# Block-sparse attention with a rational feed-forward layer: the first loads in another order, the first sampled keys copied by the vector engine, and three more buffers for the first values

## The chip, the cores and the metric

The kernel runs on one core of a Trainium2 chip. The metric is the device time of one execution in microseconds (us); three executions of the kernel before gave 875.51, 877.20 and 879.96, so the median is 877.2 us. The core has a matmul engine (PE in the profile, with its weight loads as PEld), a vector engine (DVE), a scalar engine (ACT), a general engine (POOL), and the queue SP, which here issues every DMA.

## The reference

First comes attention over `q`, `k`, `v` of shape (4, 8, 768, 64): 4 batches, 8 heads, 24 blocks of 32 rows. A block of queries sees its own block, its two neighbours, the first, the last, and three sampled blocks (`sampled_blocks`, an input); the first and the last block see everything.

```
scores = where(mask, q @ k.T / sqrt(64), -1e9);  attn = softmax(scores);  x = (attn @ v) as 3072 x 512
h = x @ w_in                                     (512 x 2048)
g = (a0 + a1*h + a2*h^2 + a3*h^3) / (1 + |b0|*|h| + |b1|*h^2 + 1e-6)
out = g @ w_out                                  (2048 x 512)
```

All inputs are float32 but the weights and the small vectors of the second part, which are float64 and are turned into float32 on the chip with integer operations (shift, or) of the vector engine.

## The kernel before

**Tiling.** The 3072 rows of `x` are 12 chunks of 256 rows (8 blocks), three chunks for each batch. A chunk's attention is done block by block (a `part` per block; the first and the last block of a batch take three parts), and then the chunk goes through 8 `unit`s (L1132), each of 256 of the 2048 columns of `w_in`. A unit is 24 matmuls into `ph` (L1150 to L1152: high and low float16 halves of `x` and of the weights), a row of scalar and vector operations for the rational function, and matmuls into `acc` (L1206 to L1208). The units' order is written out: units 0 to 3 of chunk 0, all of chunk 1, units 4 to 7 of chunk 0, then the other chunks.

**The planner.** Every piece of work is an `Op` with an engine, a price, its predecessors, the buffers that it takes from a `Ring`, and a priority. `issue` (L161 to L279) runs the list as a small simulation and emits the instructions in the order that comes out: of the operations that could start at about the same time, the one with the lower priority number goes first. So a priority is a due time, and the order of each engine's queue and of SP's is fixed when the kernel is built. Where PE has nothing to do in the first stage, `fill` (L162) puts in matmuls of an identity matrix, whose result nobody reads.

**The start.** `prep(0, ...)` (L556) loads the keys of batch 0 (six pieces of 256 KB, L545), takes their largest absolute value with ACT (`bound`, L397), makes a power of two of it (`scales`, L341: a PE transpose, a reduction and four small DVE operations) and splits, transposes and stores the keys in `kall` (`rest`, L634). In the same call it loads the values of batch 0 (L590) and takes their maximum, because the first chunk's `x` is scaled by it before it is split into float16 halves. `prep_q` does the same for 128 queries at a time, out of one buffer `ldq`; the split queries `qa` are copied to the other half of the partitions by two DMAs (`qc`, L766, L767). The key and value maxima have priorities -83.96 and -78.19.

**A part of chunk 0 or 1** (`attention`, L833). `copies` (L861) reads three block numbers from `ix` into registers of ACT and copies those blocks of `kall` into `kxs` (L866); `scores` (L913), `maxima` (DVE, L923), `exps` (ACT, L941), `turn` (PE transposes, L982), `whole` (ACT or DVE, L150), and `values` (PE, L1039) follow. The part's values come from DRAM in `load` (L1003 the three neighbours, L1005 and L1006 the first and the last block, when the buffer doesn't hold them yet, and three DMAs of L1009 for the sampled blocks, whose numbers SP reads into registers, twelve numbers for four blocks at a time). There are three value buffers `vgs`, so the load of part x waits for the values of part x-3. After four blocks, `weigh` (L1073) and `turn_x` (L1085) make a piece of `x`, and `evac_high` (L150) and `evac_low` (L1097) split it.

**The weights.** `weights()` (L414) loads 512 KB pieces into two buffers `wl`. A piece takes a conversion (ACT, POOL or DVE), and three DVE operations `pack1` to `pack3` (L447, L450, L453). Four pieces make a group of `w_in` (two units); a group then has its own scale, and three operations for each piece make its high and low halves (L150, L154, L511). A group's pieces have the priority of its first unit less 4.91: for group 0 that is -4.91. Chunk 0's attention has priorities -19 to -12.8, the set-up -70.

Of the kernel before, what the change touches and what calls it, by code (L numbers as in the profile page):

```python
# [23 lines left out]
def kernel(  # L24
# [265 lines left out]
    ix = const.tile([1, NB, 4], I32, name="ix")  # L290

# [122 lines left out]
    def weights():  # L414
# [5 lines left out]
        for u in range(NG):  # L420
            pieces += [(min(place[0, 2 * u], place[1, 2 * u]) + -4.91, 0, u, x) for x in range(NCC)]
# [101 lines left out]
    vgs = [const.tile([P, 2, 2, 2, HG * D], F16, name=f"vg{i}") for i in range(3)]  # L523
    r_kg, r_vg = Ring(range(len(kgs))), Ring(range(len(vgs)))

# [22 lines left out]
    PLAIN = B  # L548
# [4 lines left out]
    def prep(b, when):  # L553


        kv[b] = [None] * 5  # L556
        s_scr[b] = Slot(r_ks)
        first = b == 0
        n = len(units)
        k_done[b], v_done[b] = [], []  # L560
        before = {}
        if first:
            rings = [[(r_tt, "tt", p2), (r_ab, "ab", p2), (r_sq, "sq", p2)], [(r_pr, "pr", p3), (r_ld, "ld", p3)]]
        for w in ([2] if b >= QB else []) + [0, 1]:
# [7 lines left out]
            for j in range(n):  # L572
                def one(j, w=w, lds=lds, mx_tile=mx_tile):
                    prio = when(w, 0, j)
                    if first:
                        ring, tag, pool = rings[w][j // (2 + w)]
                    else:
                        ring = r_ld
# [6 lines left out]
                    def load():  # L585
                        if first:
                            nb = {"tt": 3, "pr": 4}.get(tag)
                            d["ld"] = pool.tile([P, 512], F32, name=tag, bufs=nb)
                            if w:
                                nc.sync.dma_start(out=d["ld"], in_=v[b].rearrange("h (a r) d -> (h a) (r d)", a=P // H)[:, j * 512:(j + 1) * 512])  # L590
                            else:
                                load_unit(k, b, *units[j], d["ld"])
# [24 lines left out]
            def largest(mx=mx, w=w):  # L617
# [5 lines left out]
                           finish=out_scale if w and b < PLAIN else None)  # L623
            (k_scale, v_scale)[w][b] = o
            if w and b < PLAIN:
                continue
# [11 lines left out]
    def rest(b, w, j, d, o_scale, sc, prio, before):  # L638
# [25 lines left out]
        if w == 1:  # L664
            def store():
                if kv[b][1] is None:
                    kv[b][1] = scr.tile([S, H * 2 * D], F16, name="vs")
                n = HU * 2 * D
                nc.sync.dma_start(out=kv[b][1][t * CH:(t + 1) * CH, g * n:(g + 1) * n].rearrange("(p s) c -> p s c", s=2),
                                  in_=d["hl"].rearrange("p (s j) a d -> p s (j a d)", s=2))  # L670
            v_done[b].append(Op(SY, [(650, 262144)], store, [o], prio, uses=[s_hl, s_scr[b]]))
            return
# [40 lines left out]
    def prep_q(b, t, prio, before):  # L713
# [4 lines left out]
        s_ld, s_hl, s_ps = Slot(r_ldq), Slot(r_hlq), Slot(r_sp)  # L718
# [4 lines left out]
        def load():  # L723
            d["ld"] = p1.tile([P, 512], F32, name="ldq")
# [58 lines left out]
        x = Op(TE, 445, transposes, [l], prio, takes=[s_ps], uses=[s_hl])  # L783
        x = Op(SC, 904, evac, [x], prio, takes=[d["slot"]], uses=[s_ps])
# [12 lines left out]
    def sampled_rows(x, eng=mybir.EngineType.SP):  # L797

        b, j = parts[x][:2]
        i = block(j)  # L800
        if (b, i, eng) not in rows_of:
            some = [n for n in (block(m) for m in range(j - j % 4, j - j % 4 + 4)) if n not in (0, NB - 1)]
            values = nc.values_load_multi_w_load_instructions(
                ix[0:1, some[0]:some[-1] + 1, 0:NR], engines=[eng], min_val=0, max_val=NB - 1,
                skip_runtime_bounds_check_because="clamped when ix was written")[1]
            for n, m in enumerate(some):
                rows_of[b, m, eng] = values[n * NR:(n + 1) * NR]
# [310 lines left out]
    def factors(b, u, n, after, prio):  # L1118

        def run():  # L1120
            if b not in fcs:
                fcs[b] = p2.tile([P, 4, NU], F32, name="fc")
# [254 lines left out]
```

## Time and profile before

| what | value |
|---|---|
| median of 3 executions | 877.2 us (875.51 to 879.96) |
| profiled execution: its own time | 878.83 us |
| profiled execution: span from the first to the last instruction | 877.0 us |
| mean granted PE clock, as a share of full speed | 0.976 |
| busy PE, DVE, ACT, POOL | 825.4, 729.0, 675.4, 111.4 us |
| moved by DMA | 151.16 MB, 172 GB/s over the span |

A busy time is a share over stages with different limits, so the rows below are cut into stretches of the span. Time on PE includes the fills. "Idle before" is the time in which an engine did nothing ahead of an instruction, with what ended it.

### The profile page before, as it was taken

How to read it: one execution, taken by the hardware profiler on the slowest of the kernel's cores; microseconds unless marked ns; L12 is line 12 of the kernel's file. 1: busy time of each engine (PE TensorE's matmuls, PEld its weight loads, DVE VectorE, ACT ScalarE, POOL GpSimd, SP SyncE). 2: the span in 40 equal slices, each digit the busy share in tenths (PEclk: the TensorE clock that was granted, in tenths of full speed). 3: DMA queues.
4: the chain of work that ended last, by engine and by line, in shares of the span. 5: the costliest groups of instructions: out<-in, count | busy, mean ns of one | idle time of the engine just before them, and what ended most of it. 6: DMA issues, size and time to landing. Idle time of an engine off the chain costs nothing.

```text
span 877.0 us, 27047 instructions
## 1 busy us (share of the span) xinstructions
PE 825.4 (94%) x10334; PEld 644.6 (73%) x10334; DVE 729.0 (83%) x1731; ACT 675.4 (77%) x1447; POOL 111.4 (13%) x118
## 2 busy tenths in 40 slices
PE   8988687588899999999999999999999999999997
PEld 3545566366687888888788887878778888788886
DVE  5758987999998888888887877887878887778886
ACT  6777977797787897798777788998768687767563
POOL 1124622635220000000000000000000000000000
PEclk9999898699999999999999999999999999999999
DMA  7888689586765965889755976899555965630000
GB/s 201 209 158 209 194 177 199 127 238 196 203 156 152 273 203 157 210 214 241 200 146 139 241 204 190 198 248 248 152 131 162 224 170 160 183 102 26 1 25 25
DMA packets 240209, 151.16 MB, mean 172 GB/s; under 512 B 16208, under 2 KB 222928, under 8 KB 240080
## 3 DMA queue, kind: packets, MB, share of 16 engines
q1 hardware_dynamic: 240080, 149.43, 66.4%
q8 instruction: 82, 1.34, 0.7%
q14 instruction: 47, 0.39, 0.2%
HBM read 132.07 MB, written 11.01 MB: 163 GB/s over the span
## 4 chain that ended last, share of the span: by engine, by line
PE 69%; DVE 9%; DMA 9%; ACT 5%; SPq 4%; issue 3%; POOL 1%; ACTq 0%; DVEq 0%; POOLq 0%
PE acc L1206 9%; PE ph L1150 9%; PE acc L1208 8%; PE acc L1207 8%; PE ph L1152 8%; PE ph L1151 8%; PE av L1039 5%; PE pt L982 5%; PE sp L913 5%; DMA vg<-in_v_dram 2%; DMA wl<-in_moe_w_in_dram 2%; ACT pr L941 1%; DVE pr L923 1%; SPq L1009 1%; PE sp L758 1%
## 5 line engine op out<-in xcount | busy, mean ns | idle before, releaser
L1150 PE MATMUL ph<-xh,wi 128*128 128x256 f16 x768 | 212.1, 276 | 3.7 <-DVE tt L1167 3.6
L1152 PE MATMUL ph<-xh,wi 128*128 128x256 f16 x768 | 210.9, 275 | 0.5 <-POOL wi L511 0.5
L1151 PE MATMUL ph<-xl,wi 128*128 128x256 f16 x768 | 210.9, 275 | 0.0
L1206 PE MATMUL acc<-wo_h,gh 128*128 128x512 f32 x376 | 161.2, 429 | 1.4 <-ACT wo_h L150 1.4
L1208 PE MATMUL acc<-wo_h,gl 128*128 128x512 f32 x376 | 151.2, 402 | 2.6 <-DVE gl L1195 2.6
L1207 PE MATMUL acc<-wo_l,gh 128*128 128x512 f32 x376 | 150.5, 400 | 1.5 <-POOL wo_l L464 1.5
L1174 DVE SCALAR_TENSOR_TENSOR ab<-sq,absb,ab 128x512 f32<-128x512 f32 x96 | 73.0, 760 | 51.4 <-ACT ab L1171 51.2
L1157 ACT ACTIVATE sq<-ph,fc 128x512 f32<-128x512 f32 x96 | 65.7, 684 | 63.8 <-PE ph L1152 63.3
L1150 PEld LDWEIGHTS <-wi 128*128 128x128 f16 x768 | 75.7, 99 | 28.8 <-issue 16.3
L923 DVE CUSTOM_DVE_ANT_1 pr<-sp,bias 128x256 f32<-128x256 f32 x224 | 84.6, 418 | 13.3 <-PE sp L913 11.5
L941 ACT ACTIVATE pr<-pr,st,cqb 128x256 f32<-128x256 f32 x112 | 66.1, 593 | 29.1 <-DVE st L952 29.0
L1208 PEld LDWEIGHTS acc<-wo_h,gl 128*128 128x128 f32 x376 | 71.9, 191 | 20.3 <-DVE gl L1195 3.0
L1206 PEld LDWEIGHTS acc<-wo_h,gh 128*128 128x128 f32 x376 | 72.2, 192 | 17.8 <-ACT wo_h L150 1.6
L1185 DVE SCALAR_TENSOR_TENSOR gh<-tt,par,rr 128x512 fp32r<-128x512 f32 x96 | 73.2, 763 | 13.9 <-PE acc L1207 11.2
L982 PE MATMUL pt<-ident,pr 128*128 128x128 f32 x448 | 76.5, 292 | 8.6 <-ACT pr L941 6.9
L1151 PEld LDWEIGHTS <-wi 128*128 128x128 f16 x768 | 75.7, 99 | 11.7 <-issue 3.8
L1039 PE MATMUL av<-vg,pT 128*32 128x64 f32 x3584 | 74.1, 224 | 10.2 <-DMA vg<-in_v_dram 6.2
L1152 PEld LDWEIGHTS <-wi 128*128 128x128 f16 x768 | 75.7, 99 | 10.3 <-POOL wi L511 1.0
L982 PEld LDWEIGHTS pt<-ident,pr 128*128 128x128 f32 x448 | 67.7, 205 | 20.2 <-ACT pr L941 10.1
L1207 PEld LDWEIGHTS acc<-wo_l,gh 128*128 128x128 f32 x376 | 72.3, 192 | 13.8 <-POOL wo_l L464 1.8
L1039 PEld LDWEIGHTS av<-vg,pT 128*32 128x32 f32 x3584 | 56.3, 111 | 35.2 <-issue 15.3
L150 ACT ACTIVATE pT<-pt 128x512 f32<-128x512 f32 x112 | 66.3, 592 | 15.3 <-PE pt L982 13.6
(167 smaller groups left out, 1663.3 us busy)
## 6 DMA issues: line engine op xcount, KB each, us to landing
vg<-in_v_dram SPq DMA_DIRECT2D x312, 64.0 KB, 3.3
vg<-in_v_dram SPq DMA_DIRECT2D x88, 192.0 KB, 3.7
vg<-in_v_dram SPq DMA_DIRECT2D x24, 512.0 KB, 5.5
kall<-ks SPq DMA_DIRECT2D x52, 192.0 KB, 3.3
kall<-ks SPq DMA_DIRECT2D x156, 64.0 KB, 2.2
ld<-in_k_dram SPq DMA_DIRECT2D x36, 256.0 KB, 4.5
wl<-in_moe_w_in_dram SPq DMA_DIRECT2D x32, 256.0 KB, 4.5
wl<-in_moe_w_out_dram SPq DMA_DIRECT2D x16, 512.0 KB, 5.0
```

The lines of the kernel that those rows point to most:

```text
L923: nc.vector.tensor_tensor_reduce(out=prs[x][:, g].rearrange("p (s r) -> p s r", r=BLK), in0=h["sp"][:, g].rearrange("p (s r) -> p s r", r= ...
L941: nc.scalar.activation(out=prs[x][:, g], in_=prs[x][:, g], func=AF.Exp, scale=Q["first"]["c"], bias=st[:, 6 + g:7 + g], accum_out=total if ...
L982: nc.tensor.transpose(pp[:, jj * P:(jj + 1) * P], cols, ident)
L1039: nc.tensor.matmul(av[rows, g], pT[:, 2 * g + kt, rows] if plain else pT[:, 2 * g + kt, pa_, rows], vf[:, g * HG + h4, kt * D:(kt + 1) * D ...
L1150: nc.tensor.matmul(o, wh, xh[:, :, cc], start=(cc == 0), stop=False)
L1151: nc.tensor.matmul(o, wh, xl[:, :, cc], start=False, stop=False)
L1152: nc.tensor.matmul(o, wl, xh[:, :, cc], start=False, stop=(cc == NCC - 1))
L1174: nc.vector.scalar_tensor_tensor(out=d["ab"], in0=d["sq"], scalar=absb[:, 1:2], in1=d["ab"], op0=ALU.mult, op1=ALU.add)
L1185: nc.vector.scalar_tensor_tensor(out=d["gh"], in0=d["tt"], scalar=par[:, 0:1], in1=d["rr"], op0=ALU.add, op1=ALU.mult)
L1206: nc.tensor.matmul(acc[:, t], ghs, wo_h[:, f], start=(new and e == 0), stop=False)
L1207: nc.tensor.matmul(acc[:, t], ghs, wo_l[:, f], start=False, stop=False)
L1208: nc.tensor.matmul(acc[:, t], gls, wo_h[:, f], start=False, stop=(last and e == 1))
```

## The change

It does six things.

1. The three block numbers of a block are packed into one integer (`setup`, two more DVE instructions); each part reads that one number into a register and takes the three out with shifts and masks. This holds for all parts, on SP, ACT and DVE.
2. The pieces of weight group 0 get priority -60, ahead of all attention.
3. `prep` is called for the keys of batch 0 at the start, and for the values' maximum only after the first 8 blocks have been put on the list, with priority -7. Those loads, and the key loads of batch 1, now stand behind the values of the last part of chunk 0. They go through the ring `ld`, and the rings `pr` and `ld` are no longer used by them at the start.
4. Since the values' scale isn't known then, chunk 0 takes one of its own: its two turned pieces stay in the two `ph` buffers of PSUM, ACT takes their maxima (`most`), `scales` makes a power of two, and only then are they split. Its units have factors of their own (`key`), so `factors` runs eight times instead of four for chunks 0 to 2.
5. The sampled keys of chunk 0's eight parts are copied by DVE instead of ACT. The second tile of queries gets priority -70.95 and a buffer of the `ld` ring.
6. Parts 3, 4 and 5 get value buffers of their own, in the room of `wi` where groups 2 and 3 of `w_in` come later.

Code of a path that was never taken (`PLAIN`, `vrows`, a store of the values) goes away. The diff, cut to its core:

```diff
@@ setup
+        for r in range(NR - 1, 0, -1):
+            nc.vector.scalar_tensor_tensor(out=ix[:, :, NR:NR + 1] if r == 1 else ix[:, :, r - 1:r], in0=ix[:, :, r:r + 1], scalar=float(1 << IXB), in1=ix[:, :, r - 1:r], op0=ALU.mult, op1=ALU.add)
@@ weights
-            pieces += [(min(place[0, 2 * u], place[1, 2 * u]) + -4.91, 0, u, x) for x in range(NCC)]
+            pieces += [((min(place[0, 2 * u], place[1, 2 * u]) + -4.91) if u else -60.0, 0, u, x) for x in range(NCC)]
@@ prep
-    def prep(b, when):
+    def prep(b, when, what):
...
-        before = {}
+        before = dict.fromkeys(range(3), vg_load.get(need[0] - 1)) if b < 2 else {}
@@ prep_q
-        s_ld, s_hl, s_ps = Slot(r_ldq), Slot(r_hlq), Slot(r_sp)
+        s_ld, s_hl, s_ps = Slot(r_ld if (b, t) == (0, 1) else r_ldq), Slot(r_hlq), Slot(r_sp)
@@ sampled_rows
+        if (x, eng) not in rows_of:
+            n = nc.values_load_multi_w_load_instructions(
+                ix[0:1, block(parts[x][1]), NR:NR + 1], engines=[eng], min_val=0, max_val=(1 << NR * IXB) - 1,
...
+            rows_of[x, eng] = [nc.s_assert_within((n >> r * IXB) & ((1 << IXB) - 1), min_val=0, max_val=NB - 1,
...
@@ v_plain
+        if buf < len(vgs):
+            return vgs[buf]
+        return wi[:, buf - len(vgs), NG - 2:].rearrange("p u a n -> p (u a n)").bitcast(F32).rearrange("p (h c) -> p h c", h=H)
@@ attention: copies, value buffers
+                    s_kx, dve = Slot(r_kx), x < need[0]
...
+                            times(nc.vector if dve else nc.scalar, kxs[:, s_kx.buf, r].rearrange("p h r -> p (h r)"), kall[:, bass.ds(rows[r], 1)].rearrange("p o h r -> p (o h r)"), 1.0)
+                    a = Op(VE if dve else SC, 700 if dve else 1500, copies, [o_setup, chain["edges"]], p - 1, takes=[s_kx], uses=s_kall, behind=chain.get("kx"))
...
-                s_pt, s_pT, s_vg = Slot(r_pt), Slot(r_pT), Slot(r_vg)
+                s_pt, s_pT, s_vg = Slot(r_pt), Slot(r_pT), Slot(r_vx if 3 <= x < 3 + VX else r_vg)
@@ attention: chunk 0 after its fourth and its eighth block
+        turned(G, c, e2, p)
+        def most():
...
+            bound(G["xt"], x_own[0][:, e2 // XB:e2 // XB + 1])
+        x_wait.append((G, e2, p, Op(SC, 613, most, [G["turned"]], p, uses=[G["s_ps"]])))
+        if e2 < CB - 1:
+            return
...
+        o = Op(VE, 75, largest, [w[3] for w in x_wait], p)
+        o, _ = scales(lambda: x_own[0][:, 6:7], "scx", [o], p, finish=keep, keep=lambda s, inv: x_own.append(inv))
+        x_scaled.append(o)
+        for G, e2, p, _ in x_wait:
+            evacuate(G, c, e2, p, x_own, 1, o)
@@ the list
-            return lambda w, stage, j: (-83.96, -78.19)[w] + stage * 0.5
+            return lambda w, stage, j: (-83.96, -7.0)[w] + stage * 0.5
-    prep(0, when(0))
+    prep(0, when(0), [0])
...
+            if b == 0 and t * TB == CB:
+                prep(0, when(0), [1])
-            before = prep_q(b, t, -78.95 if b == t == 0 else part_prio(x0) - (3.23 if x0 >= need[0] else 12.17), before)
+            before = prep_q(b, t, -78.95 + 8 * t if b == 0 and t < 2 else part_prio(x0) - (3.23 if x0 >= need[0] else 12.17), before)
...
+        if c < 2 and u % (WC // CH) == 0:
+            factors(b, u, WC // CH, [scale_ready[u * CH // WC], v_scale[0] if c else x_scaled[0], o_setup], place[c, u] - 1)
```

## Rows read from the trace of the kernel before

**Rows 1.** Busy time of each engine, in three stretches of the whole span: us of the stretch, then PE, PEld, DVE, ACT and POOL busy (with instructions), PE's granted clock, DMA share, GB/s.

```profile
0.00:153.00 153.00, 126.45 (x1854) 81.83 (x1855) 113.59 (x338) 117.57 (x294) 46.26 (x57) 0.93 0.83 192
153.00:240.00 87.00, 67.57 (x839) 52.88 (x837) 86.50 (x191) 72.54 (x155) 40.78 (x35) 0.88 0.70 191
240.00:850.00 610.00, 608.79 (x7522) 491.86 (x7522) 510.14 (x1177) 475.04 (x983) 24.37 (x27) 1.00 0.66 171
```

**Rows 2.** The same columns for the first stretch, cut finer.

```profile
0.00:30.00 30.00, 26.25 (x167) 12.71 (x171) 18.09 (x71) 19.33 (x45) 6.05 (x15) 1.00 0.70 188
30.00:72.00 42.00, 36.86 (x648) 21.09 (x637) 27.93 (x86) 32.85 (x93) 11.76 (x14) 0.96 0.91 191
72.00:110.00 38.00, 29.36 (x486) 20.78 (x484) 33.78 (x99) 32.75 (x80) 18.93 (x19) 0.91 0.74 203
110.00:153.00 43.00, 33.98 (x572) 27.26 (x570) 33.78 (x84) 32.65 (x77) 9.52 (x11) 0.88 0.91 187
```

**Rows 3.** The fills of PE alone (L162) in two stretches: us of the stretch, PE busy with them, clock, DMA share, GB/s.

```profile
0.00:30.00 30.00, 23.28 (x91) 1.00 0.70 188
30.00:72.00 42.00, 22.12 (x82) 0.96 0.91 191
```

**Rows 4.** PE in order of time from 28 to 74 us: start, us, line and operation, idle before it and what ended that. The first scores, the values of the last two parts of chunk 0, the second piece of `x`, the first unit.

```profile
29.77 0.23 PE L913 MATMUL sp<-kall,qa 128*32 128x96 f16 x4
...
59.91 0.91 PE L1039 MATMUL av<-vg,pT 128*32 128x64 f32 x32 [3.48 <-DMA vg<-in_v_dram]
...
63.28 0.77 PE L1039 MATMUL av<-vg,pT 128*32 128x64 f32 x32
...
65.07 0.60 PE L1085 MATMUL sp<-ident,xn 128*128 128x128 f32 x4
...
72.47 0.27 PE L1150 MATMUL ph<-xh,wi 128*128 128x256 f16 x1
```

**Rows 5.** SP's queue in order of time: the first loads of values for the maximum, the first weights, a part's values, and the last part's.

```profile
8.28 1.55 SPq L590 DMA_DIRECT2D pr<-in_v_dram  x3
9.87 1.89 SPq L590 DMA_DIRECT2D ld<-in_v_dram  x3
...
28.67 2.42 SPq L438 DMA_DIRECT2D wl<-in_moe_w_in_dram  x4
...
43.41 0.33 SPq L1003 DMA_DIRECT2D vg<-in_v_dram  x1
46.53 1.33 SPq L1009 DMA_DIRECT2D vg<-in_v_dram  x3
...
55.64 2.20 SPq L1009 DMA_DIRECT2D vg<-in_v_dram  x3
```

**Rows 6.** All DMA of the first 72 us, and two of its groups: issues, KB each, median us to landing.

```profile
DMA packets 17582, 13.65 MB, mean 190 GB/s; under 512 B 1701, under 2 KB 15268, under 8 KB 17572
...
vg<-in_v_dram SPq DMA_DIRECT2D x39, 64.0 KB, 3.7
vg<-in_v_dram SPq DMA_DIRECT2D x11, 192.0 KB, 5.1
```

**Rows 7.** Groups of ACT's instructions in the first 72 us: busy us, mean ns of one, idle before them.

```profile
L866 ACT COPY kx<-kall 128x256 f16 x30 | 9.8, 400 | 4.7 <-DVE cq L752 2.3 <-issue 2.1 <-PE sp L913 0.3
L941 ACT ACTIVATE pr<-pr,st,cq 128x256 f32<-128x256 f32 x16 | 9.4, 591 | 0.0
L150 ACT ACTIVATE pT<-pt 128x512 f32<-128x512 f32 x8 | 4.7, 586 | 0.0
...
L397 ACT ACTIVATE scrap<-pr 128x512 f16<-128x512 f32 x3 | 1.9, 624 | 0.1
...
L397 ACT ACTIVATION_READ_ACCUMULATOR scrap<-pr 128x1 f32 x3 | 0.6, 187 | 0.0
```

**Rows 8.** The same columns for DVE in the first 72 us: maxima of scores, the packing of weights, small operations, and a copy.

```profile
L923 DVE CUSTOM_DVE_ANT_1 pr<-sp,bias 128x256 f32<-128x256 f32 x16 | 6.1, 421 | 4.7 <-PE sp L913 3.0 <-ACT kx L866 1.6
L450 DVE SCALAR_TENSOR_TENSOR wi<-wl,wi 128x512 int32<-128x512 int32 x6 | 4.8, 805 | 0.1
L453 DVE SCALAR_TENSOR_TENSOR wi<-wl,wi 128x512 int32<-128x512 int32 x6 | 4.5, 748 | 0.0
...
L1097 DVE SCALAR_TENSOR_TENSOR xl<-sp,xscale,xh 128x512 f16<-128x512 f32 x2 | 1.5, 748 | 1.3 <-ACT xh L150 1.3
...
L353 DVE TENSOR_REDUCE sc<-sp 128x1 f32<-128x128 f32 x2 | 0.6, 289 | 0.5 <-PE sp L348 0.5
...
L1123 DVE SCALAR_TENSOR_TENSOR fc<-wscale,sc,coef 128x8 f32<-128x8 f32 x1 | 0.5, 460 | 0.0
...
L360 DVE TENSOR_SCALAR sc<-sc 128x1 int32<-128x1 int32 x2 | 0.3, 144 | 0.0
...
L93 DVE CAST ident<-ident 128x128 f16<-128x128 f32 x1 | 0.2, 227 | 1.4 <-POOL ident masks.py:199 1.4
```

**Rows 9.** Two lines of the timeline, POOL and DVE side by side at 71 us, and the same DVE operation at 66 us between two POOL instructions.

```profile
66.30 0.43 DVE L447 TENSOR_SCALAR wi<-wi 128x512 int32<-128x512 int32 x1
...
71.21 1.32 POOL L511 TENSOR_TENSOR wi<-dw,wi 128x512 f16<-128x512 f32 x1 [0.23 <-ACT wi L150]
71.44 1.38 DVE L447 TENSOR_SCALAR wi<-wi 128x512 int32<-128x512 int32 x1
```

**Rows 10.** ACT's timeline, the copies of the fifth and sixth part's sampled keys, behind the loading of twelve block numbers into registers.

```profile
39.30 1.94 ACT L866 COPY kx<-kall 128x256 f16 x6 [1.56 <-issue]
```

More of the change, by code (lines that the diff above doesn't have):

```diff
@@ L522 @@
     kgs = [kall[:, i * NS:(i + 1) * NS] for i in range(NB // NS)]
-    vgs = [const.tile([P, 2, 2, 2, HG * D], F16, name=f"vg{i}") for i in range(3)]
+    vgs = [const.tile([P, H, 2 * D], F32, name=f"vg{i}") for i in range(3)]
     r_kg, r_vg = Ring(range(len(kgs))), Ring(range(len(vgs)))
+    VX = 3
+    r_vx = Ring(range(len(vgs), len(vgs) + VX))
     J = (NT // 2) * TB - 1
@@ L574, in one @@
                     prio = when(w, 0, j)
[L575 to L576 removed]
+                    if first and w == 0:
+                        ring, tag, pool = rings[j // 2]
                     else:
@@ L585, in load @@
                     def load():
[L586 to L592, printed above, removed]
+                        if first and w == 0:
+                            d["ld"] = pool.tile([P, 512], F32, name=tag, bufs=3 if tag == "tt" else None)
+                            load_unit(k, b, *units[j], d["ld"])
                         else:
@@ L797, in sampled_rows @@
     def sampled_rows(x, eng=mybir.EngineType.SP):
[L799 to L807, printed above, removed]
-        return rows_of[b, i, eng]
-    def vrows(vg, kt, slot, n=1):
-        return vg[slot * BLK:(slot + n) * BLK, kt].rearrange("p g a c -> p (g a c)")
+        if (x, eng) not in rows_of:
+            n = nc.values_load_multi_w_load_instructions(
+                ix[0:1, block(parts[x][1]), NR:NR + 1], engines=[eng], min_val=0, max_val=(1 << NR * IXB) - 1,
+                skip_runtime_bounds_check_because="made of numbers clamped when ix was written")[1][0]
+            rows_of[x, eng] = [nc.s_assert_within((n >> r * IXB) & ((1 << IXB) - 1), min_val=0, max_val=NB - 1,
+                                                  skip_runtime_bounds_check_because="clamped when ix was written") for r in range(NR)]
+        return rows_of[x, eng]
     def fresh(kind, x, slot):
@@ L1035, in values @@
                     for g in range(2):
[L1036 removed]
+                        for kt in range(2):
                             for h4 in range(HG):
                                 rows = slice(h4 * BLK, (h4 + 1) * BLK)
[L1039 to L1041 removed]
@@ L1043, in two @@
-                ol = chain["vg"] = Op(SY, price, load, [o_setup] + v_done[b],
-                                      prio[m] - 0.72, takes=[s_vg], uses=[] if plain else [s_scr[b]], behind=chain.get("vg"))
+                                nc.tensor.matmul(av[rows, g], pT[:, 2 * g + kt, rows], vf[:, g * HG + h4, kt * D:(kt + 1) * D],
+                                                 start=(kt == 0 and (n == 1 or (m == 0 and g == 0))), stop=(m == n - 1 and kt == 1), skip_group_check=n > 1)
+                ol = chain["vg"] = vg_load[x] = Op(SY, price, load, [o_setup],
+                                      prio[m] - 0.72, takes=[s_vg], behind=chain.get("vg"))
@@ L1045, in two @@
                 dv = [ol]
                 o = chain["tr"] = Op(TE, 435, turn, [oexp[m]], p, behind=chain.get("tr"), takes=[s_pt], uses=[s_pr])
-                l = Op(among("t", SC, sc=478, ve=598), 0, whole if plain else high, [o], p, takes=[s_pT], uses=[s_pt])
-                if not plain:
-                    l = Op(VE, 602, low, [l], p, uses=[s_pt, s_pT])
-                o = chain["av"] = Op(TE, 560 if plain else 470, values, [l] + dv, p + 0.1, behind=chain.get("av"), takes=[s_av] if m == 0 else [], uses=[s_pT, s_vg] + ([] if m == 0 else [s_av]))
+                l = Op(among("t", SC, sc=478, ve=598), 0, whole, [o], p, takes=[s_pT], uses=[s_pt])
@@ L1051, in two @@
+                o = chain["av"] = Op(TE, 560, values, [l] + dv, p + 0.1, behind=chain.get("av"), takes=[s_av] if m == 0 else [], uses=[s_pT, s_vg] + ([] if m == 0 else [s_av]))
                 oval.append(o)
```

137 lines of the change are left out of this document (56 added, 81 removed).

## The prediction

> **What bounds the kernel now.** I read the busy times in three long stretches first, since one average over the span hides the question. From 240 to 850 us PE is busy for 608.8 of 610 us: there the matmuls are the bound, and nothing in this change touches one of them. From 153 to 240 DVE is busy for 86.5 of 87 us, PE for 67.6 [rows 1]: the vector engine is the bound while the weights are still being unpacked beside the first units. Before 153 no engine is full: DVE works 113.6 of 153 us and so leaves 39.4 idle, PE's busy time is partly fills (45.4 us in the first 72, [rows 3]), and the DMA share is 0.83 [rows 1]. So the end comes earlier by as much as DVE gets through its work of the first 240 us earlier, and that is: the idle time that the change takes out of DVE before 153, less what it adds to DVE.
>
> Where DVE idles is read from the finer stretches: 11.9 us in the first 30, 14.1 from 30 to 72, 4.2 to 110, 9.2 to 153 [rows 2]. The first 30 us go to the load of the keys and its scale. From 30 to 72 runs chunk 0's attention. ACT is the busiest there (32.9 of 42 us) and copies sampled keys for 9.8 of its time [rows 2, 7]; DMA is at a share of 0.91 with only 191 GB/s [rows 2]. In PE's order of time the first scores start at 29.77, the values of the last two parts run at 59.91 (behind a wait of 3.48 for a value load) and 63.28, the second piece of x is turned at 65.07, and the first unit starts at 72.47 [rows 4]: x would have been there some 5 us sooner, but group 0 of the weights, whose load is issued only at 28.67 [rows 5], is split last. So two chains end near 70 us, and the change shortens both.
>
> **The change, part by part.**
>
> *Loads moved.* Six value loads of 256 KB leave SP's queue at 8.28 to 11.8 [rows 5]: 3.4 us of issue, 1.5 MB ahead of the first part's values, and on ACT six maxima of 0.62 + 0.19 us (three of them in the rows), 4.9 us [rows 7]. They come back after chunk 0 (the same 3.4, 1.5 MB and 4.9 us), behind the last part's values on SP; their scale is needed only for chunk 1. Four weight pieces (2 MB, eight issues, twice the 2.42 us for four [rows 5]) move from 28.67 on to 10 to 15 us for the first two, later for the others, since there are two buffers. The queue position is exchanged rather than lengthened: value issues out, weight issues in. The second query tile's two DMAs also move ahead of the first values.
>
> *Value buffers.* Parts 3 to 5 no longer wait for the values of parts 0 to 2, at the price of two more 64 KB loads each, 0.4 MB in all. What chunk 0 must move is then 1.5 (keys) + 0.5 (queries) + 2.1 (weights) + 3.9 MB (values: six parts whole, two of 384 KB), 8.0 MB. At the 190 GB/s of the first 72 us [rows 6] that is 42 us, and 4 for the start: the last values at about 46 instead of just under 60. A sampled-block load takes 3.7 us to land [rows 6], so its latency is covered once it isn't held by buffers.
>
> *Own scale for chunk 0.* It comes behind the last values and nothing of chunk 0 covers it: two ACT maxima of 0.81 (the first beside attention), a DVE reduction, a PE transpose of about 0.3, a reduction of 0.29, four small operations of 0.14 [rows 8], then the high halves at about 0.7 on ACT and low ones at 0.75 [rows 8] for both pieces instead of one. With some five more handovers between engines, which no row prices singly and which I estimate at 0.1 to 0.3 each (the smallest operation, 0.14, is of that size), the new tail is about 4 us, of which DVE works 1.2. PE fills or waits in it.
>
> *Key copies.* ACT loses 8 of the 10 parts' copies in that stretch, 24 x 0.33 us of spacing (9.8 / 30), 7.8 us [rows 7], and its register loads (1.56 for twelve numbers [rows 10]). DVE gets 24 copies of 128x256 float16. No row shows one on DVE. Below, they can't be shorter than the smallest operation, 0.144; the cast of 128x128 took 0.227 [rows 8]; from above, a one-source operation of 128x512 32-bit elements took 0.43 [rows 9]. I take 0.25, near the cast, whose size and width are nearest: 6.0 us, ends 3.5 and 10.3. One number for each of eight parts is read: twelve held ACT for 1.56 [rows 10] and SP for 2.8 (43.74 to 46.53 [rows 5]), so 0.13 to 0.23 each, and shifts that no row shows; I take 0.24, 1.9 us for eight. The upper end, as long as ACT's whole reading each time, is 12.5 us; the lower is 1.0. The former is kept for the upper border of the range. DVE stands in order: behind each copy wait the maxima of the part before it, and ACT's exponentials behind these.
>
> *Packed numbers.* For SP the reading is spread: a block of twelve (2.8 us every four parts) becomes four of about 0.24 and some shifts, a gain of about 1.5 us in four parts against an unknown price of the shifts; SP's issue runs beside the transfers, so I count zero, and up to 1 us either way in the two chunks after. In DVE's set-up there are two more operations, 0.3 us. The four more factors are 4 x 0.46 = 1.8 us of DVE [rows 8].
>
> *Sum for DVE.* Added: 6.0 + 1.9 + 1.2 + 1.8 + 0.3 = 11.2 us. Idle taken out: about 2 in the first 30 us, where the first two weight pieces can be packed (0.43 + 0.8 + 0.75 each [rows 8, 9]) between the steps of the keys; from 30 to 72, the idle 14.1 shrinks to about 5, namely the 4 us of the new tail less what later pieces fill, plus a rest of waits, so 9; from 72 to 153, the idle 13.4 is time in which loads are awaited. The share of DMA is 0.74 from 72 to 110 and 0.91 after [rows 2]; work that comes earlier can use the slack of the first of the two, and I take 5 of the 13.4. That is 16 - 11.2, about **5 us**.
>
> The check by the first unit: by 72 DVE has worked 46.0 us [rows 2]. About 6 of these belong to weight group 1 and the third query tile, some 8 to 9 of the added work come before the first unit, and idle of about 12 to 13 remains: 46 - 6 + 8.5 + 12.5 = 61. By transfers alone it could start at 46 + 8 = 54. So I expect the first unit at about **60 us, 12 earlier**; less than half of it reaches the end, because what PE lacked there was mostly DVE's and DMA's work, not a start.
>
> The profiled execution took 878.8 us of its own time (span 877.0 and 1.8 around it), 1.6 above the median of 877.2. 878.8 - 5 = 873.8, and 1.6 lower is 872.2: I predict 872.
>
> *A rule against it.* DVE's L447 took 0.43 us at 66.30 and 1.38 at 71.44, while a POOL operation on the same kind of tile ran from 71.21 to 72.53 [rows 9]. The Trainium skill, page "SBUF — State Buffer", section "Who interferes with whom", says that a copy on the vector engine in a two-port mode and a GpSimd instruction exclude each other for a whole instruction, whoever came second waiting. By that rule, the trace agrees for L447 (1.38 against 0.43), and the copies of keys moved to DVE would meet the weight conversion on POOL, which the change puts at the same time; the sum above leaves such waits out.
>
> **The rivals.**
>
> *B, the overlap is better.* If DMA keeps a share near its 0.91 throughout, the first stretch's work (0.83 x 153 = 127 us of share, and 2 for the 0.4 MB) ends after 129 / 0.91 = 142 us, 11 earlier, and cheap copies (3.5) let DVE follow: 14 us less, 863. For it: ACT, the busiest engine from 30 to 72, is relieved. Against: there it is already 0.91 and the rate then was low. Chance 0.18.
>
> *C, the middle eats it.* The 1.5 MB of values, key loads of batch 1 and weight group 1 all come after chunk 0, so at the first unit fewer bytes have been moved (60 x 0.19 = 11.4 MB against 13.65 [rows 6]). If transfers set the pace until 153, the first unit is 12 us earlier and the stretch behind it as much longer: 875 to 879. For it: the share of 0.91 from 110 to 153; against: 0.74 before. Chance 0.22.
>
> *D, slower.* The copies on DVE run into POOL's instructions. POOL is busy for 11.8 of 42 us from 30 to 72 [rows 2], a share of 0.28; 24 copies x 0.28 x 0.95 (1.38 - 0.43) is 6.4 us, and with copies of 0.43 the addition is 10.3 + 6.4 + 1.9 + 3.3 = 21.9 against 16 of idle: 6 us more, 883. It decides from an addition of over 16 us on. For it: DVE is full from 153 on, so that nothing is forgiven; against: POOL may be early with group 0. Chance 0.18.
>
> *E, not what it says.* The weights come early but the first unit still waits until about 68 for DVE and the own scale. Idle taken out is then 10 and the end stays within 1 or 2 us: 878. Chance 0.05.
>
> **How the numbers follow.** The forecast, 868 to 876, has 0.37. A measurement of this kernel can tell about 0.5%, 4.4 us, from no change (so the borders are 872.8 and 881.6). Faster: B's 0.18 and six tenths of the forecast, 0.22, and a few of C's, 0.06, for the spread below 875; in all 0.47. Slower: D's upper part, 0.14, and tails of C and E, 0.05: 0.19. The rest, 0.34, is no change. The range goes from 860 (B with a little more than its price) to 883 (D's price); about 0.2 lies outside.
>
> **What would show it.** In the changed profile: the first weights issued before 16 us and the values for the maximum after chunk 0; no wait of the last values for a load; the first unit at 54 to 64; key copies on DVE of 0.15 to 0.43 us; DVE idle before 153 near 24 us instead of 39.4. A first unit before 64 with DMA at 0.9 and DVE idle again behind it is C; copies over 0.6 us beside POOL are D. The prediction is wrong if DVE isn't what fills the stretch up to 240, or if its queue is held by reading block numbers.

## The result and the profile after

The changed kernel takes **886.57 us** (median of six executions, 885.70 to 893.64) against 877.44 of the kernel before beside it (875.51 to 879.96): a ratio of 1.0118, 95% interval 1.0097 to 1.0140. A second measurement gave 887.14 against 879.60, ratio 1.0096 (1.0064 to 1.0129). The forecast was 872, the range 860 to 883: the sign was wrong and the time lies outside.

The rows of the changed kernel here come from the profile of that second measurement (own time 888.09, span 886.3), which is nearer its median than the first one (893.64). Lines are those of the kernel a row belongs to. First the three stretches of [rows 1]: us, then PE, PEld, DVE, ACT and POOL busy, clock, DMA share, GB/s.

```profile
0.00:153.00 153.00, 128.22 (x1883) 83.28 (x1883) 123.23 (x390) 118.17 (x286) 47.65 (x54) 0.94 0.84 198
153.00:240.00 87.00, 69.34 (x848) 53.50 (x849) 81.14 (x183) 69.24 (x148) 43.84 (x37) 0.90 0.78 200
240.00:850.00 610.00, 597.88 (x7421) 482.48 (x7421) 497.43 (x1158) 465.19 (x972) 24.91 (x28) 0.99 0.64 169
```

Up to 240 nothing is lost: PE and DVE together did more than before (DVE 204.4 us in the two stretches, 200.1 before), and DVE's idle time before 153 fell from 39.4 to 29.8 us. The last stretch is another matter. PE was busy for 608.79 of 610 us [rows 1]; now it is idle for 12.1, in a stretch of which the prediction said that nothing in the change touches it. The start, to be set against [rows 4] and [rows 5]; SP's queue, then PE in order of time:

```profile
9.59 2.53 SPq L441 DMA_DIRECT2D wl<-in_moe_w_in_dram  x4
...
50.88 1.37 SPq L596 DMA_DIRECT2D ld<-in_v_dram  x3
52.36 2.40 SPq L441 DMA_DIRECT2D wl<-in_moe_w_in_dram  x4
```

```profile
29.72 0.23 PE L901 MATMUL sp<-kall,qa 128*32 128x96 f16 x4
...
57.22 0.65 PE L1006 MATMUL av<-vg,pT 128*32 128x64 f32 x32
58.77 0.66 PE L1006 MATMUL av<-vg,pT 128*32 128x64 f32 x32
63.58 1.11 PE L1075 MATMUL ph<-ident,xn 128*128 128x128 f32 x4 [2.97 <-DVE xn L1037]
...
72.15 0.27 PE L1145 MATMUL ph<-xh,wi 128*128 128x256 f16 x1
```

The loads moved as described (weights at 9.59, the values for the maximum from 50.88), and the last values no longer wait for a load. But the first unit starts at 72.15, where it was 72.47: not at 60. So two steps of the prediction are at fault, one at 60 us and one behind 240.

### The profile page after: what moved, and what is told of

Read it like the earlier page. It is cut to its first block, busy times and chain, and to the rows that moved or that the text cites. A ratio compares the mean times of both kernels' runs of the same rounds, so it can differ in the third digit from the quotient of the medians.

```text
span 891.9 us, 28059 instructions
## 1 busy us (share of the span) xinstructions
PE 831.0 (93%) x10332; PEld 647.2 (73%) x10332; DVE 730.5 (82%) x1769; ACT 668.9 (75%) x1427; POOL 117.5 (13%) x117
## 4 chain that ended last, share of the span: by engine, by line
PE 62%; DVE 13%; DMA 9%; ACT 6%; SPq 4%; issue 3%; POOL 2%; ACTq 0%; POOLq 0%; DVEq 0%
PE acc L1201 8%; PE ph L1145 8%; PE acc L1202 8%; PE acc L1203 8%; PE ph L1147 7%; PE ph L1146 7%; PE av L1006 5%; PE pt L970 4%; PE sp L901 4%; DMA ldq<-in_q_dram 3%; DMA vg<-in_v_dram 2%; DMA wl<-in_moe_w_in_dram 2%; DVE pr L911 1%; DVE dw L453 1%; ACT pr L929 1%
## 5 line engine op out<-in xcount | busy, mean ns | idle before, releaser
L1006 PEld LDWEIGHTS av<-vg,pT 128*32 128x32 f32 x3488 | 55.3, 111 | 33.3 <-issue 10.6
L1156 ACT ACTIVATE tt<-ph,par,fc 128x512 f32<-128x512 f32 x96 | 74.9, 780 | 0.0
```

What stands on the lines that cost most here:

```text
L1006: nc.tensor.matmul(av[rows, g], pT[:, 2 * g + kt, rows], vf[:, g * HG + h4, kt * D:(kt + 1) * D], start=(kt == 0 and (n == 1 or (m == 0 an ...
L1156: nc.scalar.activation(out=d["tt"], in_=d["ph"], func=AF.Identity, scale=d["cst"][:, 3:4], bias=par[:, 2:3])
```

## The experiments

All kernels were measured in five rounds beside the kernel before. "Against U" is the difference to the first of them, U, worked out from the ratios (times 879 us). The kernels ran in four sessions on four chips, each beside the kernel before, and U in the first alone; a difference of a few microseconds against U can hold something of the chip.

| kernel | median us | ratio to before, 95% | against U |
|---|---|---|---|
| U: changed, numbers not packed | 873.69 | 0.9936 (0.9913 to 0.9958) | |
| before, numbers packed | 889.75 | 1.0113 (1.0067 to 1.0159) | |
| changed, again | 887.14 | 1.0096 (1.0064 to 1.0129) | +14.1 |
| packed for batch 0 only | 879.80 | 1.0014 (0.9997 to 1.0031) | +6.9 |
| packed for batches 1 to 3 only | 895.75 | 1.0186 (1.0163 to 1.0209) | +22.0 |
| three numbers read for each part | 876.42 | 0.9974 (0.9954 to 0.9994) | +3.3 |
| packed, query loads earlier | 890.17 | 1.0128 (1.0105 to 1.0152) | +16.9 |
| U, query loads earlier | 877.29 | 0.9985 (0.9968 to 1.0002) | +4.3 |
| U, 462 register operations added | 886.08 | 1.0084 (1.0060 to 1.0108) | +13.0 |
| U, 770 register operations added | 906.24 | 1.0294 (1.0258 to 1.0329) | +31.5 |
| U, weights in the old order | 880.05 | 1.0011 (0.9995 to 1.0027) | +6.6 |
| U, copies on ACT | 882.59 | 1.0063 (1.0036 to 1.0089) | +11.2 |
| U, without the extra buffers | 871.40 | 0.9912 (0.9896 to 0.9928) | -2.1 |
| U, later weight pieces unpacked late | 888.17 | 1.0104 (1.0077 to 1.0131) | +14.8 |

**1. The packed numbers alone.** The change without them, and the kernel before with them; in both pairs the DMAs and the work of the engines keep their order.

```
     def setup():
-        for r in range(NR - 1, 0, -1):
-            nc.vector.scalar_tensor_tensor(out=ix[...], ...)        # packs three numbers into one
 def sampled_rows(x, eng):
-        n = nc.values_load_multi_w_load_instructions(ix[0:1, block(parts[x][1]), NR:NR + 1], ...)[1][0]
-        rows_of[x, eng] = [... (n >> r * IXB) & ((1 << IXB) - 1) ... for r in range(NR)]
+        values = nc.values_load_multi_w_load_instructions(ix[0:1, some[0]:some[-1] + 1, 0:NR], ...)[1]
+        ...                                                         # twelve numbers for four blocks, as before
```

> The changed kernel, but the block numbers are read as before (twelve registers for four blocks, no packing, no shifts); the order of all other instructions on every engine is that of the changed kernel. Theory A (each part's reading, shift and mask of a packed number lengthens SP's queue, loads of later chunks come late, PE gets holes after 300 us): 872 to 879 us, PE idle between 300 and 850 us back from 10.5 to under 3 us, three sampled-block loads issued in 1.36 us instead of 1.65. Theory B (the new order of the start, with its copies on DVE and its own scale, costs the 9 us, whatever SP does): 884 to 888 us.

> The kernel before with nothing but the packed block numbers (two more DVE instructions in the set-up; all other instructions in the old order). Theory A: 884 to 890 us, with holes of PE after 300 us of 8 us or more. Theory B: 875 to 880 us.

> The changed kernel again, for a profile of an execution nearer to its median and as a base in the same job. Both theories: 885 to 888 us.

Without packing the change takes 873.69 us, 0.64% less than the kernel before, 5.6 us by the ratio: the size of the forecast gain. Packing alone makes the kernel before 1.13% slower. So one small part turned the change's sign. Where the time goes is seen in how far the units have got: the time in us at which the so many-th of the units' first matmuls (the line that reads `xh` and writes `ph` first, 768 in all) started.

```
matmul     before      U   changed   U with 770 register operations
   128     257.5   253.5    253.2    260.9
   200     324.0   320.6    324.3    334.1
   296     424.0   421.0    427.7    439.5
   392     514.3   510.1    522.3    537.1
   488     614.2   610.0    623.3    643.3
   680     800.8   795.4    809.8    832.1
   752     850.0   844.7    859.1    881.5
```

The changed kernel is 4.3 us ahead of the one before at the 128th, as U is (4.0); behind that it falls back, in holes that U lacks, the first of which ends at 289.13. From 240 to 850 its PE is idle for 12.1 us, U's for 1.8. The two longest holes (2.43 us up to 289.13 and 2.95 up to 497.56) also take PE's granted clock down: from 288.8 to 292.2 and from 497.0 to 500.4 it is 0.5 of full speed, the lower of its two levels (1.2 GHz), while U and the kernel before have 1.00 all the way from 240 to 850. The holes cost 10.3 us more than U's, and twice 3.4 us at half the clock cost an estimated 3.4: together 13.7 of the 14.4 us between the two profiled spans (886.3 and 871.9). PE in two windows of 40 us, the changed kernel and then U:

```profile
460.00:500.00 40.00, 36.04 (x441) 28.86 (x440) 28.98 (x65) 26.17 (x53) 1.11 (x2) 0.96 0.69 188
...
580.00:620.00 40.00, 39.05 (x516) 31.49 (x518) 33.00 (x79) 35.29 (x78) 3.12 (x3) 1.00 0.97 250
```

```profile
460.00:500.00 40.00, 40.00 (x481) 32.15 (x480) 32.15 (x72) 32.88 (x71) 1.39 (x2) 1.00 0.87 227
...
580.00:620.00 40.00, 40.00 (x500) 31.92 (x501) 33.10 (x81) 33.30 (x72) 1.55 (x2) 1.00 0.89 225
```

None of the engines is full in the first of those windows, nor are the transfers (in the second one the DMA share is 0.97, in U 0.89, so there they nearly are). That leaves SP's queue. A stretch of it in the changed kernel and in U: start, us from the first issue to the last one's end, line, number of issues. Between the DMAs stand the reads of numbers and the register operations, which have no row of their own here; they show as gaps, or inside a row of three sampled loads.

```profile
600.28 1.66 SPq L989 DMA_DIRECT2D vg<-in_v_dram  x3
...
609.39 0.55 SPq L758 DMA_DIRECT2D qc<-qa  x1
610.30 0.51 SPq L759 DMA_DIRECT2D qc<-qa  x1
...
612.21 0.66 SPq L870 DMA_DIRECT2D xkg<-ks  x1
613.48 1.73 SPq L873 DMA_DIRECT2D xkg<-ks  x3
615.30 0.85 SPq L1266 DMA_DIRECT2D out_dram<-ld  x2
```

```profile
595.32 0.56 SPq L756 DMA_DIRECT2D qc<-qa  x1
595.94 0.59 SPq L757 DMA_DIRECT2D qc<-qa  x1
...
597.93 0.49 SPq L871 DMA_DIRECT2D xkg<-ks  x1
601.20 2.02 SPq L874 DMA_DIRECT2D xkg<-ks  x3
603.33 0.85 SPq L1267 DMA_DIRECT2D out_dram<-ld  x2
...
608.57 1.36 SPq L990 DMA_DIRECT2D vg<-in_v_dram  x3
612.18 1.42 SPq L874 DMA_DIRECT2D kall<-ks  x3
```

The queue of the changed kernel is 12 to 14 us behind U's here: the store of the output runs at 615.30 instead of 603.33, the copies of the queries at 609.39 instead of 595.32. Three sampled loads take 1.66 to 1.73 us instead of 1.36 to 1.42 (U's row of 2.02 holds one slow issue, of 0.96). What packing saves is seen in U between 597.93 + 0.49 and 601.20: 2.78 us, the reading of twelve numbers, once in four parts. A full issuing queue is what the Trainium skill lists as one kind of DMA-bound kernel ("Perfetto Trace Analysis", section "What "DMA-bound" means": the issuing engine's sequencer track is solid DMA slices, which are the generation of descriptors and not the movement of data). The trace agrees in part: the DMA share is 0.64 to 0.66 in the last stretch, but SP's rows fill 396 of the 501 us from 300 us to its last issue, and reads, register operations and waits fill the rest.

**2. Which part of the packing.** Packed numbers for batch 0's parts alone, for the others alone, and a read for each part that fetches its three numbers as they are, with no shifts.

```
+    ixp = const.tile([1, NB, 1], I32, name="ixp")      # in the first two: a tile of its own for the packed numbers
 def sampled_rows(x, eng):
+        if x >= KX:          # in the second kernel: if x < KX
+            ...              # twelve numbers for four blocks
         ...                  # packed
```
```
-        n = nc.values_load_multi_w_load_instructions(ix[0:1, block(...), NR:NR + 1], ...)[1][0]
-        rows_of[x, eng] = [... (n >> r * IXB) & ((1 << IXB) - 1) ...]
+        rows_of[x, eng] = nc.values_load_multi_w_load_instructions(ix[0:1, i:i + 1, 0:NR], ...)[1]
```

> The changed kernel with packed numbers for the 22 parts of batch 0 whose keys lie in kall, and numbers read twelve at a time for all later parts; the order of all other instructions is that of the changed kernel. If SP's longer queue in the later batches is the cost (theory A, its place): 871 to 877 us, PE idle from 300 to 850 us under 3 us. If the cost arises at the start, where DVE and ACT read packed numbers too, and is only seen later: 884 to 888.

> The reverse: packed numbers for the later batches alone. Theory A, its place: 884 to 889 us with 7 us or more of PE idle from 300 to 850 us. Otherwise 871 to 878.

> The changed kernel's order, no packing: each part reads its own three numbers with one instruction, without shifts and masks (88 reads on SP as with packing, 0 register operations instead of 770). If the shifts and masks between the DMAs are what lengthens the queue: 871 to 877 us. If the larger count of reads is: 882 to 888.

The loss comes mostly from the later batches, +22.0 against +6.9, but this split is not clean: neither time lies in a range that was expected, the two do not add up to the +14.1 of both, and packing for batch 0 alone adds nothing to SP's queue after 300 us (the table in 4). These two kernels alone hold the tile `ixp`, and in them alone the DMA share from 240 to 850 us is up, 0.71 and 0.68 where every other kernel here has 0.63 to 0.66, at the same 169 to 172 GB/s. If that costs both the same, it is (6.9 + 22.0 - 14.1) / 2 = 7.4 us, and -0.5 and +14.6 are left for the packing; this is an estimate, and since no run has the tile alone, it stays open. With a read for each part but no shifts the loss is 3.3 us: the number of reads is not the cause of the 14. Each read of one packed number leaves a gap of 0.59 us before its loads (0.26 without a read, one register operation included); a read of three numbers, without register operations, leaves 0.92 (0.20 without a read).

**3. A theory that fell: the late query loads.** In the changed kernel DVE waits in order for the queries' low halves, which POOL makes; the theory was that POOL is late because their load was issued late. Waits of DVE and of PE between 300 and 850 us (us in all, times, the longest), changed kernel, then U's DVE:

```profile
DVE hlq L394 <- POOL hlq L154: 11.9, 5, 5.3
...
PE av L1006 <- ACT pT L150: 4.2, 3, 3.0
```

```profile
DVE hlq L392 <- POOL hlq L154: 3.5, 3, 1.2
```

So these loads were given an earlier place, in the changed kernel and in U (the planner then moves some of DVE's and ACT's work too, alike in both):

```
-        o_ld = Op(SY, [...], load, (), prio - 1, takes=[s_ld], behind=before)
+        o_ld = Op(SY, [...], load, (), prio - (3 if b else 1), takes=[s_ld], behind=before)
```

> The changed kernel, packed numbers kept, with one edit: the query loads of batches 1 to 3 are given a priority 2 earlier, so that they stand some 10 to 25 places further ahead in the order of the sync engine's queue; the other engines' orders stay nearly the same. Theory A1 (the longer queue costs through the query loads alone: they are issued late, POOL's low halves come late, DVE waits in order for them): most of the 13 us between the changed kernel and the unpacked one come back, 876 to 880 us, and DVE's wait for POOL's low halves of the queries falls from 12 to 14 us towards 4. Theory A2 (the longer queue is late everywhere, so that moving the queries ahead makes other loads late): 885 to 890 us.

> The changed kernel without packing (873.7 us when it ran before), with the same earlier query loads. If what is left of DVE's waits for the low halves (3.5 us there) is on the path, 870 to 873 us; if the loads moved behind them are as near to being late, 874 to 878. By A1 this kernel and the packed one with the same edit end within 4 us of each other; by A2 they stay some 13 us apart.

The wait went away, the loss did not: 890.17, and 0.0143 x 879 = 12.6 us between the two kernels, as theory A2 has it. In the packed one the next waits are ACT's, for the maxima of other loads, and PE's for ACT:

```profile
DVE hlq L394 <- POOL hlq L154: 2.4, 3, 1.2
...
ACT scrap L400 <- DMA ld<-in_q_dram: 6.5, 2, 4.8
...
ACT scrap L400 <- DMA ld<-in_v_dram: 5.8, 3, 4.3
ACT scrap L400 <- DMA ld<-in_k_dram: 3.8, 3, 2.1
...
PE av L1006 <- ACT pT L150: 4.6, 2, 3.7
```

So it was not this one load that was late: ACT's waits for loads whose maxima it takes stay, 16.1 us of them (14.3 in the changed kernel, 3.2 in U). Even in U, moving the queries forward, with the other moves that this brought, cost 4.3 us.

**4. The register operations by themselves.** U, which has no shifts or masks on SP, computes every number of a sampled load anew with operations that leave it as it was: 770 of them, as many as in the changed kernel and at the same places, or 462. All else keeps its order.

```
+    def longer(r, n):
+        n = (n & 31) if r == 0 else ((n + 32) & 31)     # in the second kernel: n & 31
+        return nc.s_assert_within(n, ...)
...
-        in_=ks[bass.ds(rows[r], 1)]
+        in_=ks[bass.ds(longer(r, rows[r]), 1)]          # and likewise for the values
```

> The unpacked kernel (873.7 us when it ran before), with the register operations of the packed one put on the sync engine and nothing else: every sampled load computes its block number anew with one mask, or an addition and a mask, that leave the number as it was; 770 register operations, as many as in the changed kernel, at the same places. Theory S (the register operations lengthen the sync engine's queue, and that alone makes the loss): 885 to 889 us, a triple of sampled loads issued in 1.66 us instead of 1.36. Rival R (it is the reading or the packing itself, or the place of the reads): 872 to 877.

> The same with the masks alone: 462 register operations, three in a triple of sampled loads instead of five. Theory S with a loss in proportion: 873.7 + 0.6 x 13, about 881 to 883 us. If the loss has a threshold (loads hidden until the queue is full), 874 to 878; by rival R no change, 872 to 877.

Rival R is out: U with nothing but these operations is 31.5 us slower, with 462 of them 13.0. Theory S had the cause, and sizes that were too small (885 to 889 and 881 to 883). The measure is what they add to SP's queue. Over 300 to 840 us (some 55 threes of value loads and 54 of key loads) I take the medians of those rows' lengths and the sum of the gaps ahead of them:

```
                                      values   keys   gaps   added to SP   against U
U                                      1.36    1.41   60.3
three numbers read for each part       1.37    1.41   61.8       2.0          +3.3
U, 462 register operations             1.48    1.54   62.4      15.7         +13.0
changed                                1.67    1.73   47.5      21.5         +14.1
packed for batch 0 only                1.37    1.42   59.1      -0.1          +6.9
packed for batches 1 to 3 only         1.66    1.73   49.2      22.7         +22.0
U, 770 register operations             1.66    1.70   60.2      32.1         +31.5
```

(For the changed kernel: 55 x 0.31 + 54 x 0.32 + 47.5 - 60.3 = 21.5.) Where the operations stand in the later batches, from 0.65 of SP's added time to all of it reaches the end; the +6.9 of batch 0 alone is not explained by this measure, and 2.0 against +3.3 is within the noise. In part, the 770 cost more in U than in the changed kernel because U still reads twelve numbers at a time, while the changed kernel saves 12.8 us of gaps; but SP's times are 10.6 us apart and the ends 17.4. U with 770 operations also starts its first unit later, at 75.9, and is 7.4 us behind U at the 128th matmul. How SP's time gets there is seen in ACT's waits for loads whose maxima it takes, from 300 to 850 us: 3.2 us in U, 14.0 with 462 operations, 14.3 in the changed kernel, 23.4 with 770. The kernel before goes the same way with packing, less fully (4.5 and 21.0 us of such waits): 0.29 and 0.31 longer and 9.4 us fewer gaps, 23.3 us of SP, for 9.9 at the end.

**5. The other parts of the change**, each taken back in U:

```
-  pieces += [((min(...) + -4.91) if u else -60.0, 0, u, x) ...]     # weights in the old order
+  pieces += [(min(...) + -4.91, 0, u, x) ...]
-  s_kx, dve = Slot(r_kx), x < need[0]                               # copies on ACT
+  s_kx, dve = Slot(r_kx), False
-  s_vg = Slot(r_vx if 3 <= x < 3 + VX else r_vg)                    # without the extra buffers
+  s_vg = Slot(r_vg)
+  prio = prio if (kind, u) == (0, 0) else max(prio, 7.2)            # later weight pieces late (the unpacking; the loads keep their priority)
```

> The changed kernel without packing, with weight group 0 loaded at its old priority (after chunk 0's loads); the first values' late maximum, the copies on DVE and the buffers stay. If the earlier weights bring the gain, the first unit comes later than 72 us and the end is 4 to 10 us later, 878 to 884. Rival: since the first unit did not come earlier with them (71.5 against 72.5), the order of the weight loads is worth nothing and the end is 872 to 877.

> The first experiment's kernel with the key copies of chunk 0 on ACT again; the planner orders anew. If the copies on DVE are part of the gain (ACT relieved by 7.8 us while DVE has idle time to give): 876 to 882 us. If DVE's added work costs as much as ACT's relief brings: within 2 us of the first experiment's 874; if it costs more, 868 to 871.

> The changed kernel without packing and without the three extra value buffers (all sampled values turn in the first three); the rest stays. If the buffers are worth what the prediction says of them (the last values of chunk 0 held by buffers until just under 60 us), the values of parts 3 to 7 wait again and the end comes 2 to 6 us later than with them, 876 to 880 us. Rival: the first unit waits for the weights' scales on DVE's queue and not for the values, and the end stays within 2 us, 872 to 876.

> The first experiment's kernel, and the unpacking of all weights but group 0 is put on the list only after the first unit (their loads stay early). Theory C (the first unit is not earlier because DVE's queue stands 4.7 us behind group 1's weights, with chunk 0's second piece of x waiting behind it): second piece of x on PE at 58 to 61 us instead of 65, first unit at 66 to 70 us instead of 74.6. Rival D (x is late for another reason, the last values or ACT): first unit still at 73 to 76. For the end, if DVE's total work and the transfers set it: within 3 us of the first experiment either way.

The early weights are worth 6.6 us and the copies on DVE 11.2; the planner reorders other work with each, so these are the parts' prices in this kernel, not of the instructions alone. The extra buffers are worth nothing: without them the median is 871.40, the best of all, 0.88% under the kernel before; its interval and U's overlap, so against U no more than a hint (871.40 is under both ranges that were expected). The last kernel was made for the first unit, below: with later weights out of DVE's way the second piece of `x` came at 59.80 instead of 62.83 and the first unit at 67.78 instead of 71.45, yet the end was 14.8 us later; DVE then worked only 66.64 us from 72 to 153 instead of 74.28.

## Why the prediction was wrong

**Packed numbers: the step that failed.** "For SP the reading is spread ... a gain of about 1.5 us in four parts against an unknown price of the shifts; SP's issue runs beside the transfers, so I count zero, and up to 1 us either way in the two chunks after." The gain was there: 12.8 us of gaps in 540 us. The price was more: 0.31 us for each three loads, twice in a part, 34.3 us over the same stretch, 21.5 net, and 14 at the end. Two things were missed. A register value that is an expression is worked out again at each use, here five operations for each three loads, in every batch to the end (770 on SP, for 154 threes): the step counted one chunk or two. And "beside the transfers" does not hold for a queue that is itself nearly full. The rows of SP that the step rests on are of the first 72 us, and the busy PE after 240 was taken as a proof that nothing else was near. An engine at 99.8% with a neighbour that is nearly late looks the same as one with ample slack.

**The first unit at about 60: failed**, rival E's picture. The forecast counted work and transfers, not the queues' order. DVE in the changed kernel, between the two pieces of `x`:

```profile
55.60 0.20 DVE L1033 RECIPROCAL sm<-sm 128x8 f32<-128x8 f32 x1
60.39 0.43 DVE L450 TENSOR_SCALAR wi<-wi 128x512 int32<-128x512 int32 x1 [4.59 <-POOL wi L154]
60.85 0.69 DVE L453 SCALAR_TENSOR_TENSOR wi<-wl,wi 128x512 int32<-128x512 int32 x1
61.58 1.01 DVE L456 SCALAR_TENSOR_TENSOR wi<-wl,wi 128x512 int32<-128x512 int32 x1
62.51 0.41 DVE L450 TENSOR_SCALAR wi<-wi 128x512 int32<-128x512 int32 x1
62.85 0.68 DVE L1037 TENSOR_TENSOR xn<-av,sm 128x512 f32<-128x512 f32 x1
```

DVE stands 4.59 us before group 1's weights, whose load was issued at 52.36 only, while the values of chunk 0 were done at 58.77 + 0.66. Behind them `x` waits until 62.85. The own scale was put at "about 4 us"; from the turn of the second piece to the first unit it is 72.15 - 63.58 = 8.6, because its small DVE operations take turns with those of the next queries' scale, and its ACT maximum (64.96) comes behind those of other loads. In the last kernel of 5 DVE has no such wait, and the second piece and the first unit come 3.0 and 3.7 us earlier than in U; so the wait is real (the first unit's start differs by 2.9 us between the changed kernel's own two profiles, 72.15 and 75.0, so its size is rough), and taking it away like this pays nothing.

**What held.** The gain without packing is 5.6 us where the sum said 5, but that was luck: its terms fared worse. U's three stretches:

```profile
0.00:153.00 153.00, 127.37 (x1883) 83.03 (x1884) 120.55 (x388) 117.54 (x285) 48.21 (x54) 0.94 0.85 199
153.00:240.00 87.00, 68.64 (x843) 53.30 (x843) 80.35 (x181) 69.47 (x148) 43.29 (x36) 0.90 0.77 198
240.00:850.00 610.00, 608.19 (x7522) 493.05 (x7520) 512.30 (x1180) 474.68 (x985) 25.78 (x28) 1.00 0.65 169
```

Idle taken out of DVE before 153 is 7.0 in U (153 - 120.55 = 32.45, against 39.4), not 16; by the sum's own stretches, up to 30, 72 and 153 us, it is 0.8, -0.5 and 6.7 where the sum had 2, 9 and 5. From 153 to 240, where the prediction has DVE full, U's is idle for 6.65 us (0.5 before), so DVE's idle time before 153 does not set the end as the prediction's first step has it. And the added 11.2 is nowhere in the total, which goes from 729.0 to 727.4 us. Of it, the 24 copies took 5.5 us at 0.24 each in the changed kernel and 3.9 at 0.22 in U (6.0 at 0.25 were forecast), and the four factors 0.8 instead of 1.8; against that, the same 48 small operations of L940 (L952 before) fell from 17.4 to 12.8. The sum came right by errors that cancel. Value buffers: no wait for a load, as forecast, but the last values at 57 to 59 us and not 46; their loads were issued by 50.82 and no wait for one stands before them, so attention's own chain held them and not the transfers.

**The rivals.** B and C spoke of the early stretches; D's collision was not met, since the copies ran between 28.45 and 46.4 us and POOL was idle there but for the end of two instructions, the first row below:

```profile
27.18 1.78 POOL L1100 COPY kx<-kall 128x512 f16<-128x512 f16 x2 [1.66 <-DVE cq L741]
```

```profile
27.51 0.98 DVE L453 SCALAR_TENSOR_TENSOR wi<-wl,wi 128x512 int32<-128x512 int32 x1
28.45 0.86 DVE L152 COPY kx<-kall 128x256 f16 x3
29.23 0.69 DVE L456 SCALAR_TENSOR_TENSOR wi<-wl,wi 128x512 int32<-128x512 int32 x1
29.83 0.57 DVE L152 COPY kx<-kall 128x256 f16 x3
```

Beside it L453 took 0.98 instead of 0.69, and of the first three copies the first took 0.60, where all others took 0.21 to 0.23: once, and for 0.3 to 0.4 us each. That is what the rule cited there says (the Trainium skill, "SBUF — State Buffer", section "Who interferes with whom": one of the two waits while the other holds the shared ports); the trace agrees for the first copy, which ends just behind POOL's second one (29.05 and 28.96). D's time, 883, was nearest to the result, by a mechanism that did not act. No rival had SP's queue in it, though the prediction's last sentence names "reading block numbers" as a way to be wrong, for DVE's queue alone. Two slips of the working changed nothing: the 12.5 us kept for the upper border are not in D's price, which became that border, and the chances of faster add up to 0.46, not 0.47.

## What to carry to other kernels

Read the queue that issues the DMAs like an engine, over the whole span: sum its rows, its gaps, and ask what a few tenths of a microsecond in each issue add up to. Arithmetic on register values is paid at every use on the queue that uses it; read the number ready-made where the queue is full. A change of several parts is best timed with each part alone: here one part's 14 us hid a gain of 5.6, and another part was worth nothing.

## What the runs showed of the hardware that was not expected

A register operation between SP's DMAs costs 0.06 to 0.08 us: of those that belong to three loads, the first stands ahead of the row (a gap of 0.26 instead of 0.20) and the others lengthen it, two by 0.12 and four by 0.30. Reading one number costs 0.33 (a gap of 0.59 against 0.26), three 0.72 (0.92 against 0.20), twelve 2.6 (2.78 against 0.20). On DVE three copies of 128x256 float16 take 0.49 us in U, a copy every 0.13 us with 0.22 for one, and 0.57 to 0.78 in the changed kernel with the shifts between them (0.86 beside POOL); ACT took 1.03 us for the same three. In the changed kernel PE's granted clock fell to 0.5 for 3.4 us at the end of each of its two longest holes behind 240 us (2.43 and 2.95 us), so these two cost more than their length.
